# Operands of VectorE moved from SBUF to PSUM in an attention and feed-forward kernel, row additions moved from GpSimd to VectorE, and a second bank for the second products

## The chip, the cores and the metric

One core of one Trainium2 chip. The metric is the device time of one execution in microseconds, the median of three runs. A tile is 128 partitions wide (`P`); PSUM has eight banks of 512 float32 values per partition.

## The reference

Three blocks in a row, float32, batch 2, 768 positions, width 512.

1. Attention with 8 heads of 64. Query and key rows get a bucket from the signs of six projections; only pairs in the same bucket count; then softmax and the product with the values.
2. `u = x + real(fft2(x))` over positions and width; a norm of each row of `u`; `relu(un @ w_ch1) @ w_ch2` with 2048 hidden columns; the result is added to `u`.
3. A gated block: `gelu(x @ w_in)` in two halves, a norm of the second, a product over positions with `w_sg`, a bias, the gate, `w_out`, and the residual.

```python
    X = np.fft.fft(np.fft.fft(x, axis=1), axis=2)
    u = x + np.real(X)
    un = (u - mean(u)) / np.sqrt(var(u) + 1e-06)
    ch = np.maximum(un @ w_ch1, 0.0) @ w_ch2
    return u + ch
```

The weights of blocks 2 and 3 come as 64-bit floats.

## The kernel before, in words

**Precision.** Products of blocks 2 and 3 use pairs of float16, a high and a low part; three products stand for one. Hence the many pairs of a ScalarE copy (`AF.Copy`, high part) and a VectorE subtraction (low part).

**Weights** (`weight`, lines 197 to 239). A load brings 64-bit words into the tile `wide`. Three VectorE instructions make one 32-bit float of the two halves of a word: line 219 shifts and masks the high half, line 220 adds the sign bit, line 221 adds bits of the low half. `w1` is merged in pieces of 1024 columns, `w2` in 16 pieces of 512, `w_in` and `w_out` in pieces of 256. Before the change `t`, the partly merged word, lies in its final place in SBUF. Then ScalarE squares and sums (line 223), and lines 232 and 234 make the high and low parts.

**Attention** (`attention`, lines 360 to 491) goes through 96 items (batch, head, 128 query rows). For each: scores on TensorE (line 387), maximum on VectorE (line 397), exponential on ScalarE (line 399), the float16 pair (lines 244 or 246, and 251 on GpSimd), a transposing DMA (line 438), and the products with the values (lines 455 to 457) into the bank `pav`.

**Transform** (`fft`, lines 494 to 605), per batch. `XU[b]` holds the 768 rows as six tiles; tile `t` and tile `HT + t` belong together. The fold makes their sum `e` and difference `o` and folds the columns (lines 520 to 533). Step 1 (lines 536 to 560) and step 2 (lines 562 to 574) are products with tables. Step 2 gives `p` and `q` in PSUM; ScalarE scales `q` to `qs`; lines 586 and 587 make `d = p - q` and `u = p + q`. They are added to the rows: lines 590 and 591 to tile `A` on VectorE, 595 and 596 to tile `Bt` on GpSimd. Then statistics (lines 599 and 600).

**Norm** (`norm`, lines 607 to 636): a reciprocal root by three Newton steps (`rsqrt`, lines 108 to 118) on one value per row, 6 columns at once for batch 0 and 2 at a time for batch 1. The rows are centred and scaled by a power of two (line 631), split, and transposed by DMA. The block 3 norm calls the same `rsqrt` with one column.

**Feed-forward** (`ch`, lines 639 to 697): chunks of 256 rows. First products (line 657) go into banks of `self.pp`, then lines 663 and 664 make the hidden pair. Second products (line 674) add up 48 matmuls in one bank with the tag `c2`, and line 678 adds the result to `XU`. A chunk has two such groups, one for each 128 rows.

**Order.** `build` merges generators by weights: batch 0's attention with `w1`; then a stream with the rest of the attention and batch 1's transform, a stream with batch 0's transform and feed-forward, and one with `w2`; then batch 1's feed-forward with the block 3 weights; then block 3. `TileContext(nc, schedule_with_timeline_sim=True)` then orders the instructions of each engine by its own model of their times.

**PSUM banks.** While the middle streams run with attention, `self.pp` alternates between two banks; `pa` (tag `pav`) and `pc` (tag `c2`) have one each, and four hold scores. When attention ends, the four go to `pp3`, and `self.pp` rotates over six; `pa` stays allocated with no further use.

Of the kernel before, what the change touches and what calls it, by code (L numbers as in the profile page):

```python
# [9 lines left out]
F32 = mybir.dt.float32  # L10
FR = mybir.dt.float32r
F16 = mybir.dt.float16
I32 = mybir.dt.int32
AF = mybir.ActivationFunctionType
ALU = mybir.AluOpType
# [4 lines left out]
DM, DF, DG = 512, 2048, 1024  # L20
P = 128
# [7 lines left out]
NL = DM // 2 + 1  # L29
# [17 lines left out]
LN1 = (True, False)  # L47
# [54 lines left out]
class Kern:  # L102
    def __init__(self, tc, I, out):
        self.tc, self.nc, self.I, self.out = tc, tc.nc, I, out
        self.W = {}


    def rsqrt(self, pool, x, n):
        nc = self.nc
        y = pool.tile([P, n], F32, tag="rs_y", name="rs_y", bufs=2)  # L110
        t = pool.tile([P, n], F32, tag="rs_t", name="rs_t", bufs=2)
        nc.vector.tensor_scalar(out=y.bitcast(I32), in0=x.bitcast(I32), scalar1=1, scalar2=None, op0=ALU.logical_shift_right)
        nc.vector.tensor_scalar(out=y.bitcast(I32), in0=y.bitcast(I32), scalar1=-1.0, scalar2=float(0x5F3759DF), op0=ALU.mult, op1=ALU.add)
        for _ in range(3):
            nc.vector.tensor_tensor(out=t, in0=y, in1=y, op=ALU.mult)
            nc.vector.scalar_tensor_tensor(out=t, in0=t, scalar=-0.5, in1=x, op0=ALU.mult, op1=ALU.mult)
            nc.vector.scalar_tensor_tensor(out=y, in0=t, scalar=1.5, in1=y, op0=ALU.add, op1=ALU.mult)
        return y

# [77 lines left out]
    def weight(self, pool, nm, src, regions, spare, c, q):  # L197

        nc = self.nc
        wide = src.dtype == mybir.dt.int64  # L200
        src = src.bitcast(I32) if wide else src
        sub = WSUB.get(nm, 4)
        m = c // sub
        n = len(regions)
        s, i = self.sc[nm]
        acc = pool.tile([P, 8], F32, tag="wacc", name="wacc", bufs=1)
        tot = pool.tile([P, 1], F32, tag="wm", name="wm", bufs=1)
        for j in range(n):
            if not wide:
                q.dma_start(out=regions[j], in_=src[:, j * c:(j + 1) * c])  # L210
                yield 0.3
            for hf in range(sub if wide else 0):
                o = j * c + hf * m
                x = self.stp.tile([P, 2 * m], I32, tag="wide", name="wide", bufs=self.wb)
                q.dma_start(out=x, in_=src[:, 2 * o:2 * (o + m)])
                xv = x.rearrange("p (n w) -> p n w", w=2)
                lo, hi = xv[:, :, 0], xv[:, :, 1]
                t = regions[j][:, hf * m:(hf + 1) * m].bitcast(I32)
                nc.vector.tensor_scalar(out=t, in0=hi, scalar1=3, scalar2=0x3FFFFFFF, op0=ALU.logical_shift_left, op1=ALU.bitwise_and)
                nc.vector.scalar_tensor_tensor(out=t, in0=hi, scalar=-0x40000000, in1=t, op0=ALU.bitwise_and, op1=ALU.bitwise_or)  # L220
                nc.vector.scalar_tensor_tensor(out=t, in0=lo, scalar=29, in1=t, op0=ALU.logical_shift_right, op1=ALU.bitwise_or)  # L221
                yield 0.0029 * m
            nc.scalar.activation(spare[:, 0:c], regions[j], AF.Square, accum_out=acc[:, j:j + 1])
            yield 0.0005 * c
        nc.vector.tensor_reduce(tot, acc[:, 0:n], axis=AX.X, op=ALU.add)
        self.norm_pow2(tot, 2.0 ** 54, s, i, self.pc if nm == "w2" else None)
        yield 1.0
        views = []
        dst = spare
        for j in range(n):  # L230
            d = dst[:, 0:c].bitcast(F16).rearrange("p (t c) -> p t c", t=2)
            nc.scalar.activation(d[:, 0, :], regions[j], AF.Copy, scale=i)
            yield 0.0005 * c
            nc.vector.scalar_tensor_tensor(out=d[:, 1, :], in0=regions[j], scalar=i, in1=d[:, 0, :], op0=ALU.mult, op1=ALU.subtract)
            views.append(d)
            dst = regions[j]
            yield 0.0005 * c
        self.W[nm] = views
        self.spare = dst
# [254 lines left out]
    def fft(self, fp, b, unT, up=None):  # L494

        nc, I = self.nc, self.I
# [14 lines left out]
        s, i = self.sx[b]  # L511
        h = DM // 2
# [2 lines left out]
        oe = fp.tile([1, NL], F32, tag="row", name="oe")  # L515
        for t in range(HT):
            A, Bt = XU[:, t], XU[:, HT + t]
            e = fp.tile([P, DM], F32, tag="k2", name="fe", bufs=4)
            o = fp.tile([P, DM], F32, tag="k2", name="fo", bufs=4)
            nc.vector.tensor_tensor(out=e, in0=A, in1=Bt, op=ALU.add)  # L520
            nc.gpsimd.tensor_tensor(out=o, in0=A, in1=Bt, op=ALU.subtract)
            nc.vector.tensor_tensor(out=e[:, 1:h], in0=e[:, 1:h], in1=e[:, DM - 1:h:-1], op=ALU.add)
            nc.scalar.activation(ee[:, t, 0], e[:, 0:NL], AF.Copy, scale=i)
            nc.vector.scalar_tensor_tensor(out=ee[:, t, 1], in0=e[:, 0:NL], scalar=i, in1=ee[:, t, 0], op0=ALU.mult, op1=ALU.subtract)
            if t == 0:
                nc.vector.tensor_tensor(out=oe[:, 1:h], in0=o[0:1, 1:h], in1=o[0:1, DM - 1:h:-1], op=ALU.add)
                nc.vector.tensor_copy(oe[:, 0:1], o[0:1, 0:1])
                nc.vector.tensor_copy(oe[:, h:h + 1], o[0:1, h:h + 1])
                nc.scalar.activation(oeh[0:1, 0], oe, AF.Copy, scale=i[0:1])
                nc.vector.scalar_tensor_tensor(out=oeh[0:1, 1], in0=oe, scalar=i[0:1], in1=oeh[0:1, 0], op0=ALU.mult, op1=ALU.subtract)  # L530
            nc.gpsimd.tensor_tensor(out=o[:, 1:h], in0=o[:, 1:h], in1=o[:, DM - 1:h:-1], op=ALU.subtract)
            nc.scalar.activation(oo[:, t, 0], o[:, 0:h], AF.Copy, scale=i)
            nc.vector.scalar_tensor_tensor(out=oo[:, t, 1], in0=o[:, 0:h], scalar=i, in1=oo[:, t, 0], op0=ALU.mult, op1=ALU.subtract)
            yield 2.0
# [45 lines left out]
        for t in range(HT):  # L580
            p = step2(t * P, P, yc, cl, True)
            q = step2(t * P, P, ys, sl, False)
            qdu = fp.tile([P, 3, NL], F32, tag="k3", name="qdu", bufs=2)
            qs, d, u = (qdu[:, j] for j in range(3))
            nc.scalar.activation(qs, q[:, 0:NL], AF.Copy, scale=s)
            nc.vector.scalar_tensor_tensor(out=d, in0=p[:, 0:NL], scalar=s, in1=qs, op0=ALU.mult, op1=ALU.subtract)
            nc.vector.scalar_tensor_tensor(out=u, in0=p[:, 0:NL], scalar=s, in1=qs, op0=ALU.mult, op1=ALU.add)
            yield 1.6
            A, Bt = XU[:, t], XU[:, HT + t]
            nc.vector.tensor_tensor(out=A[:, 0:NL], in0=A[:, 0:NL], in1=d, op=ALU.add)  # L590
            nc.vector.tensor_tensor(out=A[:, NL:DM], in0=A[:, NL:DM], in1=u[:, h - 1:0:-1], op=ALU.add)
            if t == 0:
                nc.scalar.activation(d[0:1], d3, AF.Copy)
                nc.scalar.activation(u[0:1], d3, AF.Copy)
            nc.gpsimd.tensor_tensor(out=Bt[:, 0:NL], in0=Bt[:, 0:NL], in1=u, op=ALU.add)
            nc.gpsimd.tensor_tensor(out=Bt[:, NL:DM], in0=Bt[:, NL:DM], in1=d[:, h - 1:0:-1], op=ALU.add)
            for n, X in enumerate((A, Bt)):
                st = fp.tile([P, 6], F32, tag="bst", name="bst", bufs=2)
                nc.vector.bn_stats(st, X)
                nc.vector.bn_aggr(mv[:, t, n], st)  # L600
            yield 2.0
            if not LN1[b]:
                yield from self.norm(fp, up, b, unT, mv, (t,))
# [3 lines left out]
    def norm(self, fp, up, b, unT, mv, ts):  # L607
        nc, XU = self.nc, self.XU[b]
        t0, w = ts[0], 2 * len(ts)
        x, e, i, s = (fp.tile([P, w], F32, tag=f"ln{j}", name=f"ln{j}", bufs=1 if LN1[b] else 2) for j in range(4))  # L610
        nc.vector.tensor_scalar(out=x.rearrange("p (a c) -> p a c", c=2), in0=mv[:, t0:ts[-1] + 1, :, 1], scalar1=EPS, scalar2=None, op0=ALU.add)
        nc.vector.tensor_scalar(
            out=e.bitcast(I32), in0=x.bitcast(I32), scalar1=24, scalar2=23, op0=ALU.logical_shift_right, op1=ALU.logical_shift_left
# [1 line left out]
        nc.vector.tensor_scalar(  # L615
            out=i.bitcast(I32), in0=e.bitcast(I32), scalar1=-1.0, scalar2=float(190 << 23), op0=ALU.mult, op1=ALU.add
        )
        rs = self.rsqrt(fp, x, w)
        nc.vector.reciprocal(s, i)
        nc.vector.tensor_tensor(out=self.tok[b][:, 2 * t0:2 * t0 + w], in0=rs, in1=s, op=ALU.mult)  # L620
        yield 0.9
        for t in ts:
            A, Bt = XU[:, t], XU[:, HT + t]
# [15 lines left out]
    def ch(self, hp, b, unT, step, tags=None):  # L639
        nc = self.nc  # L640
# [26 lines left out]
        def c2(n, j, f):  # L667
            w2 = self.W["w2"]
            if f == 0:
                self.c2t = self.pc.tile([P, 512], F32, tag="c2", name="c2")  # L670
            ps = self.c2t
            wv = w2[f // 2].rearrange("p t (k c) -> p t k c", k=2)[:, :, f % 2, :]
            for m, (a, w) in enumerate(HH):
# [141 lines left out]
    def build(self):  # L815
# [3 lines left out]
        with ExitStack() as ctx:  # L819
# [47 lines left out]

            def second():
                yield from att
                c_att.close()  # L870
                c_s2.close()
                pp3 = c_ps.enter_context(tc.tile_pool(name="pp3", bufs=4, space=PSUM))
# [113 lines left out]
```

## Time and profile before

| | |
|---|---|
| median of 3 runs | 722.25 us (721.98 to 722.77) |
| the profiled execution | 724.48 us, span 722.7 us |
| TensorE busy | 645.0 us (89%), 4828 matmuls |
| VectorE busy | 503.9 us (70%), 1095 instructions |
| ScalarE busy | 329.8 us (46%), 517 instructions |
| GpSimd busy | 273.7 us (38%), 232 instructions |
| mean granted TensorE clock | 0.943 |

Busy time is the sum of the spans of an engine's instructions. PE is TensorE, DVE VectorE, ACT ScalarE, POOL GpSimd. A busy engine that waits inside an instruction counts as busy. The granted clock is the share of TensorE's full speed.

### The profile page before, as it was taken

The numbers are of one execution on the slowest core, as the hardware profiler recorded it, in microseconds if no ns is written. First come the engines' busy times: TensorE is split into PE (matmuls) and PEld (weight loads), VectorE is DVE, ScalarE is ACT, GpSimd is POOL, SyncE is SP. The second block draws the span as 40 slices with busy tenths as digits, with TensorE's granted clock in tenths as the row PEclk, the third lists the DMA queues.
The fourth block names the chain that finished last, engine by engine and source line by source line (L and its number), as shares of the span: only waits on it lengthen the run. The fifth ranks groups of instructions, "written<-read, shape, count | busy, mean of one in ns | idle before, by whom it ended". The sixth has DMA issues, their size and how long they took to land.

```text
span 722.7 us, 12521 instructions
## 1 busy us (share of the span) xinstructions
PE 645.0 (89%) x4828; PEld 421.8 (58%) x4828; DVE 503.9 (70%) x1095; ACT 329.8 (46%) x517; POOL 273.7 (38%) x232
## 2 busy tenths in 40 slices
PE   3788987976876578999999999979999999999997
PEld 0666677764563357658865766736668444444443
DVE  6999598658999997745435694867562266777663
ACT  5766687764664556745632421423642044222110
POOL 2568588879486465536455041000000012111000
PEclk8899999996886879999999999989999999999999
DMA  8969787999798989737563036552000012011334
GB/s 310 312 182 213 140 175 143 204 202 259 158 235 169 212 193 211 140 67 152 101 128 108 2 60 221 125 148 91 1 1 1 1 35 53 15 29 18 86 88 117
DMA packets 182428, 92.24 MB, mean 128 GB/s; under 512 B 166240, under 2 KB 167008, under 8 KB 181344
## 3 DMA queue, kind: packets, MB, share of 16 engines
q1 hardware_dynamic: 181792, 91.30, 55.0%
q8 instruction: 38, 0.62, 0.4%
q10 hardware_dynamic: 576, 0.14, 0.1%
q14 instruction: 22, 0.18, 0.1%
HBM read 39.50 MB, written 3.15 MB: 59 GB/s over the span
## 4 chain that ended last, share of the span: by engine, by line
PE 56%; DVE 21%; DMA 12%; POOL 4%; issue 3%; ACT 2%; SPq 0%; DVEq 0%; POOLq 0%; ACTq 0%
PE c L674 13%; PE c L657 12%; PE gi L739 9%; PE sg L762 6%; PE s L387 4%; PE go L779 4%; DMA wide<-w_in 3%; DMA et<-eh 3%; DMA wide<-w 3%; DVE nm L397 2%; DVE w L221 2%; DVE w L220 2%; POOL eh L251 2%; DVE k L258 1%; PE y L542 1%
## 5 line engine op out<-in xcount | busy, mean ns | idle before, releaser
L251 POOL TENSOR_TENSOR eh<-e,eh 128x768 f16<-128x768 f32 x80 | 143.4, 1796 | 53.7 <-ACT eh L244 51.0
L657 PE MATMUL c<-unT,w 128*128 128x256 f16 x1152 | 136.8, 277 | 4.2 <-DVE h L664 4.2
L674 PE MATMUL c<-w,h 128*128 128x512 f16 x576 | 131.8, 384 | 5.3 <-DVE xu L678 5.3
L657 PEld LDWEIGHTS <-w 128*128 128x128 f16 x1152 | 113.0, 99 | 22.6 <-issue 5.3
L387 PE MATMUL s<-k,q 128*128 128x384 f32 x384 | 108.1, 413 | 17.8 <-ACT k L282 7.4
L399 ACT ACTIVATE e<-s,nm 128x768 f32<-128x768 f32 x96 | 85.3, 896 | 55.3 <-DVE nm L397 44.7
L397 DVE TENSOR_REDUCE nm<-s 128x1 f32<-128x768 f32 x96 | 90.3, 948 | 22.6 <-PE s L387 21.5
L674 PEld LDWEIGHTS <-h 128*128 128x128 f16 x576 | 56.2, 99 | 69.6 <-issue 9.2
L755 POOL TENSOR_TENSOR vh<-gv,vh 128x512 f16<-128x512 f32 x12 | 13.9, 1156 | 214.0 <-ACT vh L754 214.0
L387 PEld LDWEIGHTS s<-k,q 128*128 128x128 f32 x384 | 72.0, 211 | 30.1 <-ACT k L282 8.3
L455 PE MATMUL pav<-V,et 128*128 128x65 f16 x480 | 56.4, 199 | 19.2 <-DMA et<-eh 13.8
L664 DVE SCALAR_TENSOR_TENSOR h<-c,h 128x256 f16<-128x256 f32 x96 | 39.8, 419 | 36.3 <-ACT h L663 35.8
L246 POOL TENSOR_SCALAR eh<-e 128x768 f16<-128x768 f32 x48 | 47.9, 999 | 36.8 <-ACT e L399 30.7
L455 PEld LDWEIGHTS <-et 128*128 128x128 f16 x480 | 46.0, 102 | 26.1 <-DMA et<-eh 17.7
L456 PE MATMUL pav<-V,et 128*128 128x64 f16 x480 | 56.2, 197 | 0.0
L457 PE MATMUL pav<-V,et 128*128 128x65 f16 x480 | 56.2, 199 | 0.0
L456 PEld LDWEIGHTS <-et 128*128 128x128 f16 x480 | 46.5, 101 | 7.7 <-issue 6.9
L739 PE MATMUL gi<-in,xT 128*128 128x512 f16 x216 | 50.5, 379 | 0.0
L663 ACT ACTIVATE h<-c 128x256 f16<-128x256 f32 x96 | 34.6, 377 | 34.6 <-PE c L657 34.2
L739 PEld LDWEIGHTS <-xT 128*128 128x128 f16 x288 | 28.2, 98 | 35.0 <-issue 1.1
L457 PEld LDWEIGHTS <-et 128*128 128x128 f16 x480 | 46.5, 101 | 1.5 <-issue 0.8
L762 PE MATMUL sg<-vh,sg 128*128 128x512 f16 x180 | 40.8, 379 | 0.0
(198 smaller groups left out, 1009.9 us busy)
## 6 DMA issues: line engine op xcount, KB each, us to landing
wide<-w SPq DMA_DIRECT2D x8, 1024.0 KB, 8.9
wide<-w SPq DMA_DIRECT2D x16, 512.0 KB, 4.3
x<-qk SPq DMA_DIRECT2D x16, 384.0 KB, 4.5
k<-q SPq DMA_DIRECT2D x26, 192.0 KB, 4.1
wide<-w_in SPq DMA_DIRECT2D x16, 256.0 KB, 3.5
vst<-v SPq DMA_DIRECT2D x8, 396.0 KB, 5.3
y<-ot SPq DMA_DIRECT2D x12, 256.0 KB, 2.3
q<-q SPq DMA_DIRECT2D x13, 192.0 KB, 3.9
```

Source lines behind the costliest of these rows:

```text
L246: self.nc.gpsimd.tensor_scalar(out=out, in0=src, scalar1=scale, scalar2=1.0, op0=ALU.mult, op1=ALU.mult)
L251: (self.nc.vector if eng == "D" else self.nc.gpsimd).tensor_tensor(out=out, in0=a, in1=b, op=ALU.subtract)
L387: nc.tensor.matmul(s[:, hf, 0:HS], q[:, qs], k[:, hf * HS:(hf + 1) * HS], start=n == 0, stop=n == len(pairs) - 1)
L397: nc.vector.tensor_reduce(nm, x["s"], axis=AX.XY, op=ALU.max, negate=True)
L399: nc.scalar.activation(e.rearrange("p (a c) -> p a c", a=2), x["s"], AF.Exp, bias=nm)
L455: nc.tensor.matmul(pv[:, qt, 0:65], et[:, kb, :], V[:, hl, kb, 64:129], start=kb == 0, stop=False)
L456: nc.tensor.matmul(pv[:, qt, 0:64], et[:, kb, :], V[:, hl, kb, 0:64], start=False, stop=False)
L457: nc.tensor.matmul(pv[:, qt, 0:65], et[:, NT + kb, :], V[:, hl, kb, 64:129], start=False, stop=kb == NT - 1)
L657: nc.tensor.matmul(ps[:, 0:step], w[:, a, fo], uT[:, 4 * u + kc, o * P:o * P + step], start=m == 0, stop=m == 11)
L674: nc.tensor.matmul(ps, hs[n, f][:, a, j * P:(j + 1) * P], wv[:, w, :], start=f + m == 0, stop=f == NF - 1 and m == 2)
L739: nc.tensor.matmul(ps, xT[:, 4 * a + kc, :], w_in[kc][:, w, half * DM:(half + 1) * DM], start=n == 0, stop=n == 11)
L762: nc.tensor.matmul(ps, w_sg[kt][:, w, t * P:(t + 1) * P], vh[b][:, kt, a, :], start=n == 0, stop=n == 17)
```

## The change

Six edits.

- `weight`: for `w2` alone the partly merged word lies in a tile of 512 columns with the tag `c2` in PSUM; the third instruction writes the final place in SBUF.
- `rsqrt`: the temporary `t` may be handed in, and the factors are taken in another order (`x*y` times `y` for `y*y` times `x`). `norm` hands in PSUM: `x` and `t` lie in one bank of `self.pp`.
- Fold: `e` lies in a bank of `self.pp` with 257 columns, the other 255 go into `er` in SBUF, by an addition of their own.
- Step 2: `d` and `u` are written over `q` and `p` in their banks.
- The additions to `Bt` go to VectorE.
- `ch`: once the attention is over, every other second product takes the bank of `pa`.

```diff
-    def rsqrt(self, pool, x, n):
+    def rsqrt(self, pool, x, n, t=None):
...
-        t = pool.tile([P, n], F32, tag="rs_t", name="rs_t", bufs=2)
+        t = pool.tile([P, n], F32, tag="rs_t", name="rs_t", bufs=2) if t is None else t
...
-            nc.vector.tensor_tensor(out=t, in0=y, in1=y, op=ALU.mult)
-            nc.vector.scalar_tensor_tensor(out=t, in0=t, scalar=-0.5, in1=x, op0=ALU.mult, op1=ALU.mult)
+            nc.vector.tensor_tensor(out=t, in0=x, in1=y, op=ALU.mult)
+            nc.vector.scalar_tensor_tensor(out=t, in0=t, scalar=-0.5, in1=y, op0=ALU.mult, op1=ALU.mult)
...
-                t = regions[j][:, hf * m:(hf + 1) * m].bitcast(I32)
+                to = regions[j][:, hf * m:(hf + 1) * m].bitcast(I32)
+                t = self.pc.tile([P, 512], F32, tag="c2", name="wt")[:, 0:m].bitcast(I32) if nm == "w2" else to
...
-                nc.vector.scalar_tensor_tensor(out=t, in0=lo, scalar=29, in1=t, op0=ALU.logical_shift_right, op1=ALU.bitwise_or)
+                nc.vector.scalar_tensor_tensor(out=to, in0=lo, scalar=29, in1=t, op0=ALU.logical_shift_right, op1=ALU.bitwise_or)
...
-            e = fp.tile([P, DM], F32, tag="k2", name="fe", bufs=4)
+            e = self.pp.tile([P, 512], F32, tag="p", name="fe")[:, 0:NL]
+            er = fp.tile([P, h - 1], F32, tag="k2", name="fer", bufs=4)
...
-            nc.vector.tensor_tensor(out=e, in0=A, in1=Bt, op=ALU.add)
+            nc.vector.tensor_tensor(out=e, in0=A[:, 0:NL], in1=Bt[:, 0:NL], op=ALU.add)
+            nc.vector.tensor_tensor(out=er, in0=A[:, NL:DM], in1=Bt[:, NL:DM], op=ALU.add)
...
-            nc.vector.tensor_tensor(out=e[:, 1:h], in0=e[:, 1:h], in1=e[:, DM - 1:h:-1], op=ALU.add)
+            nc.vector.tensor_tensor(out=e[:, 1:h], in0=e[:, 1:h], in1=er[:, ::-1], op=ALU.add)
...
-            qdu = fp.tile([P, 3, NL], F32, tag="k3", name="qdu", bufs=2)
-            qs, d, u = (qdu[:, j] for j in range(3))
+            qs = fp.tile([P, NL], F32, tag="k3", name="qs", bufs=2)
+            d, u = q[:, 0:NL], p[:, 0:NL]
...
-            nc.gpsimd.tensor_tensor(out=Bt[:, 0:NL], in0=Bt[:, 0:NL], in1=u, op=ALU.add)
-            nc.gpsimd.tensor_tensor(out=Bt[:, NL:DM], in0=Bt[:, NL:DM], in1=d[:, h - 1:0:-1], op=ALU.add)
+            nc.vector.tensor_tensor(out=Bt[:, 0:NL], in0=Bt[:, 0:NL], in1=u, op=ALU.add)
+            nc.vector.tensor_tensor(out=Bt[:, NL:DM], in0=Bt[:, NL:DM], in1=d[:, h - 1:0:-1], op=ALU.add)
...
-        x, e, i, s = (fp.tile([P, w], F32, tag=f"ln{j}", name=f"ln{j}", bufs=1 if LN1[b] else 2) for j in range(4))
+        e, i, s = (fp.tile([P, w], F32, tag=f"ln{j}", name=f"ln{j}", bufs=1 if LN1[b] else 2) for j in range(3))
+        ps = self.pp.tile([P, 512], F32, tag="p", name="lnp")
+        x, r = (ps[:, 8 * j:8 * j + w] for j in range(2))
...
-        rs = self.rsqrt(fp, x, w)
+        rs = self.rsqrt(fp, x, w, r)
...
-                self.c2t = self.pc.tile([P, 512], F32, tag="c2", name="c2")
+                self.c2n += 1
+                other = self.att_over and self.c2n % 2
+                self.c2t = (self.pa if other else self.pc).tile([P, 512], F32, tag="pav" if other else "c2", name="c2")
...
                 yield from att
+                self.att_over = True
```

## Rows read from the trace of the kernel before

**Rows 1.** Busy time by stage: stretch, its length, engines, granted clock, DMA share, GB/s.

```profile
164.00:290.00 126.00, 92.37 (x828) 64.89 (x827) 116.32 (x186) 70.32 (x109) 81.43 (x63) 0.81 0.92 207
290.00:440.00 150.00, 150.00 (x1313) 104.90 (x1314) 87.13 (x198) 65.16 (x109) 65.57 (x52) 1.00 0.46 94
440.00:579.00 139.00, 132.88 (x879) 86.52 (x878) 78.26 (x227) 44.80 (x92) 0.00 (x0) 0.98 0.25 73
579.00:723.00 144.00, 139.86 (x648) 63.18 (x646) 94.04 (x313) 35.28 (x53) 13.87 (x12) 1.00 0.22 55
```

**Rows 2.** Groups of VectorE, 164 to 290 us: busy us, mean ns, idle before.

```profile
L221 DVE SCALAR_TENSOR_TENSOR w<-wide,w 128x512 int32<-128x512 int32 x16 | 17.7, 1104 | 0.1
L220 DVE SCALAR_TENSOR_TENSOR w<-wide,w 128x512 int32<-128x512 int32 x16 | 16.8, 1051 | 0.1
L219 DVE TENSOR_SCALAR w<-wide 128x512 int32<-128x512 int32 x16 | 9.0, 560 | 2.7 <-DMA wide<-w 2.7
...
L524 DVE SCALAR_TENSOR_TENSOR ee<-fe,ix,ee 128x257 f16<-128x257 f32 x3 | 4.1, 1370 | 0.0
...
L520 DVE TENSOR_TENSOR fe<-xu 128x512 f32<-128x512 f32 x3 | 4.0, 1342 | 0.0
L591 DVE TENSOR_TENSOR xu<-xu,qdu 128x255 f32<-128x255 f32 x3 | 3.7, 1233 | 0.0
...
L590 DVE TENSOR_TENSOR xu<-xu,qdu 128x257 f32<-128x257 f32 x3 | 3.0, 994 | 0.0
L116 DVE SCALAR_TENSOR_TENSOR rs_t<-rs_t,ln 128x6 f32<-128x6 f32 x3 | 2.9, 954 | 0.0
...
L522 DVE TENSOR_TENSOR fe<-fe 128x255 f32<-128x255 f32 x3 | 1.9, 655 | 0.0
...
L117 DVE SCALAR_TENSOR_TENSOR rs_y<-rs_t,rs_y 128x6 f32<-128x6 f32 x3 | 1.4, 480 | 0.0
...
L586 DVE SCALAR_TENSOR_TENSOR qdu<-p,sx,qdu 128x257 f32<-128x257 f32 x3 | 1.4, 468 | 0.0
```

**Rows 3.** Timeline, 184 to 189 us: start us, length us, engine, instruction.

```profile
184.28 0.68 DVE L220 SCALAR_TENSOR_TENSOR w<-wide,w 128x512 int32<-128x512 int32 x1
...
186.54 1.63 POOL L251 TENSOR_TENSOR eh<-e,eh 128x768 f16<-128x768 f32 x1
186.59 2.13 DVE L221 SCALAR_TENSOR_TENSOR w<-wide,w 128x512 int32<-128x512 int32 x1
```

**Rows 4.** TensorE's waits, 440 to 585 us: total us, times, longest.

```profile
PE c L674 <- DVE xu L678: 5.3, 2, 4.4
PE gi L739 <- DVE xu L678: 0.8, 1, 0.8
```

**Rows 5.** Timeline of VectorE ahead of TensorE's longer wait.

```profile
481.94 0.29 DVE L219 TENSOR_SCALAR in<-wide 128x256 int32<-128x256 int32 x1 [0.70 <-DMA wide<-w_in]
...
482.61 0.75 DVE L678 SCALAR_TENSOR_TENSOR xu<-c,tok,xu 128x512 f32<-128x512 f32 x1
```

**Rows 6.** Groups of VectorE over the whole span, for prices.

```profile
L766 DVE SCALAR_TENSOR_TENSOR t<-t,bB,gu 128x512 f32<-128x512 f32 x12 | 9.0, 752 | 0.4
...
L678 DVE SCALAR_TENSOR_TENSOR xu<-c,tok,xu 128x512 f32<-128x512 f32 x12 | 9.0, 746 | 23.7 <-PE c L674 23.7
...
L765 DVE TENSOR_TENSOR t<-sg,gB 128x512 f32<-128x512 f32 x12 | 8.3, 692 | 15.3 <-PE sg L762 15.3
...
L116 DVE SCALAR_TENSOR_TENSOR rs_t<-rs_t,ve 128x1 f32<-128x1 f32 x36 | 5.7, 159 | 1.2
```

**Rows 7.** Group of GpSimd, 164 to 290 us.

```profile
L596 POOL TENSOR_TENSOR xu<-xu,qdu 128x255 f32<-128x255 f32 x3 | 2.5, 821 | 1.4 <-DVE qdu L586 1.4
```

**Rows 8.** Timeline of VectorE, batch 0's step 2 and root.

```profile
202.65 0.47 DVE L587 SCALAR_TENSOR_TENSOR qdu<-p,sx,qdu 128x257 f32<-128x257 f32 x1
...
205.48 0.99 DVE L591 TENSOR_TENSOR xu<-xu,qdu 128x255 f32<-128x255 f32 x1
...
235.28 0.14 DVE L611 TENSOR_SCALAR ln<-mv 128x6 f32<-128x6 f32 x1
...
255.77 0.17 DVE L117 SCALAR_TENSOR_TENSOR rs_y<-rs_t,rs_y 128x6 f32<-128x6 f32 x1
```

More of the change, by code (lines that the diff above doesn't have):

```diff
@@ L105, in __init__ @@
         self.W = {}
-    def rsqrt(self, pool, x, n):
+        self.c2n, self.att_over = 0, False
+    def rsqrt(self, pool, x, n, t=None):
         nc = self.nc
         y = pool.tile([P, n], F32, tag="rs_y", name="rs_y", bufs=2)
-        t = pool.tile([P, n], F32, tag="rs_t", name="rs_t", bufs=2)
+        t = pool.tile([P, n], F32, tag="rs_t", name="rs_t", bufs=2) if t is None else t
         nc.vector.tensor_scalar(out=y.bitcast(I32), in0=x.bitcast(I32), scalar1=1, scalar2=None, op0=ALU.logical_shift_right)
```

## The prediction

> **What bounds the kernel now.** I read the busy table by stage first, cut where the TensorE row of the page changes character. Four stages matter [rows 1]. From 290 us on TensorE sets the time: it is busy 150.0 of 150, 132.9 of 139 and 139.9 of 144 us, at a granted clock of 1.00, 0.98 and 1.00. From 164 to 290 us it isn't: it works 92.4 of 126 us, at 0.81. There batch 1's attention, batch 0's transform and the merging of the words of `w2` run together, and VectorE is busy 116.3 of 126 us. The DMA share is 0.92 too, which makes some 116 us of transfers. Before 164 us nothing is changed: `w1` still merges in SBUF. So the reader should look for two things: what VectorE does between 164 and 290, and where TensorE still waits after 440.
>
> The groups of VectorE in that stretch answer the first [rows 2]. Instructions with two SBUF tensors take far more than their size asks: 1.05 and 1.10 us for 512 elements, 0.99 and 1.23 us for 257 and 255, 0.95 us for six elements (line 116). In the same stretch line 586, one PSUM and one SBUF tensor of 257, takes 0.468. The timeline shows why [rows 3]: the same merge step takes 0.68 us alone, and 2.13 us where it starts 0.05 us behind a GpSimd add that itself lasts 1.63. VectorE stands until GpSimd lets go. [...]
>
> The second: after 440 us TensorE's waits for VectorE come to 5.3 us at line 674, in two pieces, the longer 4.4, and 0.8 at line 739 [rows 4]. Line 674 wants the only `c2` bank, which line 678 must empty. Line 678 stands in VectorE's queue among the merges of `w_in`, and those wait for their loads [rows 5].
>
> **The change part by part**, in the stretch from 164 to 290, in VectorE time. Prices for one PSUM and one SBUF tensor: 0.692 us for 512 elements without a scalar pointer, 0.746 with one, so the pointer costs 0.054 [rows 6]; 0.468 for 257 with a pointer, so 0.41 without.
>
> Words of `w2`, 16 halves: lines 220 and 221 now cost 16.8 + 17.7 = 34.5 us; 32 times 0.692 is 22.1, so -12.4. Line 219 (0.560) has no row with a PSUM output. Its ends are no change and the full 0.692; I take the latter, as nearest in size: +2.1. Together -10.3. All 16 share the one `c2` bank, so the steps of two halves can't overlap any more; VectorE runs them in turn anyway, and nothing else wants that bank until `w2` is ready.
>
> Fold, three tiles: line 520 (1.342) becomes two adds, both still with two SBUF inputs. Between 0.41 alone and the 0.99 of line 590 I take 0.99, since GpSimd works beside them: 6 x 0.99 - 4.0 = +1.9. Line 522 falls from 0.655 to 0.41 (-0.7 in three), line 524 from 1.370 to 0.468 (-2.7). Together -1.5.
>
> Row additions: lines 590 and 591 fall from 0.994 and 1.233 to 0.41 each (-1.8 and -2.5). Six additions come from GpSimd, 6 x 0.41 = +2.5. Together -1.8. GpSimd loses them, three of 0.82 us [rows 7] and three of about that width, some 5 us, which shortens its hold on the others. VectorE's queue gets them ahead of the statistics, which had waited for GpSimd.
>
> Root: each of its three-input steps then has one SBUF tensor. Lines 116 and 117 (0.954 and 0.480) fall to the 0.159 of the same step where nothing disturbs it [rows 6]: -2.4 - 1.0 = -3.4. The other order of factors changes no count.
>
> Sum: -10.3 - 1.5 - 1.8 - 3.4 = -17.0 us of VectorE. What a VectorE write to PSUM costs isn't in the trace. At best it is nothing. At worst the steps that write PSUM (lines 220, 522 and 116) stay at what they take now; they are 5.7 + 0.7 + 2.4 = 8.8 us of the sum, so the relief is 8.2 to 17.0. I take 17.0: a read from PSUM shows no surcharge, 0.746 (line 678) against 0.752 for the like with two SBUF tensors (line 766) [rows 6].
>
> How much of it shortens the stage? VectorE idles 9.7 us of 126, so it alone would let all 17 through. The transfers don't shrink: 0.92 of 126 us is 116, so about 10 us is what there is before they bind. Attention's transposes could slide into the next stage, where the share is 0.46 [rows 1]. I take -10, with -3 and -17 as ends. From 290 on TensorE is full, so its work simply starts earlier and the gain stays.
>
> Two banks for second products: `att_over` is set before batch 1's part, so the 5.3 us of line 674 go; the other bank has been empty for a whole group of 48 matmuls. The loads of `w_in` then are late for nobody on TensorE until the last stage. The 0.8 us at line 739 I leave. -5.3, with -3 and -6.1 as ends.
>
> After 384 us, batch 1's transform runs beside a full TensorE. Its VectorE savings are worth nothing there, and its longer held banks may cost: six banks rotate, so I put +1 for all of them (0 to +4).
>
> Total -10 - 5.3 + 1 = -14.3. The profiled execution took 724.48 us (span 722.7), 2.2 over the median of 722.25. It should come to 710.2, and the median to 708.0.
>
> **The rivals.**
>
> Transfers hold the stage (0.17). If the 0.92 is already what the transfers can do with their waits, VectorE's relief turns into waiting for loads, and only the banks remain: 722.25 - 5.3 + 1 = 718. For it speaks the share; against it that after 290 us, with the same transposes, it is 0.46, and that VectorE is just as full.
>
> PSUM writes are dear (0.08): a relief of 8.2 instead of 17.0, and the same 10/17 of it gained, is 4.8; with the banks -9.1, or 713. [...]
>
> Banks held too long (0.10), the one that ends slower. In the stage at issue two banks serve the fold, both steps of the transform, the root and attention's norm. The pair `p`, `q` was free when line 587 ended, at 203.1; now it is held past line 591, which ended at 206.5, and two more additions of 0.41: 4.2 us longer [rows 8], three times 12.6. The root holds a bank from 235.3 to 255.9 [rows 8], when first products want both: up to 4. The fold's first sum may wait for one tile's chain, 1.34 + 0.66 + 1.37 = 3.4. TensorE takes its instructions in order, so attention waits behind. That is 20 us, against 15.3 saved: about 727 if none hides. It decides once more than 15.3 of the 20 are exposed. Against it: TensorE is idle 33.6 us of this stage already, and such waits fall into that.
>
> It doesn't do what it says (0.05): the stretching stays, and only the additions count, 2.1 + 1.9 + 2.5 = +6.5, against -5.3: some 722 to 724.
>
> **How the numbers follow.** The forecast has 0.60. About 0.2% is what a measurement of this kernel can tell from no change. Faster takes the forecast, the dear writes and most of the first rival, 0.83; the same, the unchanged case and the bad end of the first, 0.07; slower, the held banks, 0.10. The range: below, the whole 17 and 6.1, 722.25 - 23.1 = 699; above, the first rival at 718 with a little more of the bank waits, 719. Outside lie the held banks, the unchanged case and a sliver below.
>
> **What would show it.** Right: `w2`'s line 220 and 221 steps near 0.69 us with hardly any above 0.8; lines 522, 524, 590, 591 at 0.41 to 0.47; root steps near 0.16; six more additions on VectorE and none of these on GpSimd; the first second product some 10 us earlier than 289; no wait for line 678 at line 674. Wrong: these fall but the stage stays 126 us long and `w2`'s first step waits for its load (transfers); the steps that write PSUM stay near 1 us (dear writes); TensorE waits in the transform for lines 590 to 596 of the new kernel (banks). The order of instructions on each queue is drawn up anew for the changed kernel, which can shift a few us either way.

## The result, and the profile after

The changed kernel takes 713.93 us (median of 4 runs, 712.84 to 714.82) against 722.12 for the kernel before beside it (719.14 to 722.77). The ratio is 0.9861, with an interval of 0.9823 to 0.9899: faster by 1.4%, which is 10 us by the ratio and 8 between the medians. The forecast was 708.0 with a range of 699 to 719. The profiled execution took 714.82 us, its span is 713.0.

Busy time by stage, the kernel after, in the cuts of [rows 1]:

```profile
164.00:290.00 126.00, 95.75 (x915) 69.11 (x914) 111.17 (x201) 78.84 (x118) 81.24 (x65) 0.86 1.10 226
290.00:440.00 150.00, 148.51 (x1245) 101.98 (x1244) 83.51 (x210) 56.26 (x98) 47.19 (x37) 1.00 0.42 86
440.00:579.00 139.00, 133.69 (x882) 86.85 (x880) 79.43 (x239) 48.22 (x96) 0.00 (x0) 0.99 0.22 60
579.00:713.00 134.00, 130.20 (x604) 58.82 (x601) 88.65 (x291) 30.91 (x48) 13.87 (x12) 0.99 0.24 58
```

From 290 us on TensorE sets the time as it did. In the first stretch it works 95.75 us at a granted clock of 0.86, before 92.37 at 0.81 (means of two levels: in cuts of 0.5 us the clock is 0.50 or 1.00 in 239 of 252 before and in 242 of 252 after). Busy time times clock estimates its work at full speed (the clock is a mean over the whole stretch, idle time included): 82.3 us against 74.8. So some 7.5 us more of it is done by the same moment, and is spared later, where the clock is 0.99 to 1.00. The busy time is only 3.4 us longer; the rest is the higher clock. It isn't that this execution was ahead already: cut 3 us earlier, from 161 to 287 us, the kernel after has the same 95.75 us at 0.86.

Groups of VectorE in the stretch from 164 to 290 us of the kernel after (against [rows 2]):

```profile
L221 DVE TENSOR_SCALAR wt<-wide 128x512 int32<-128x512 int32 x16 | 11.0, 686 | 1.5 <-DMA wide<-w 1.4
L222 DVE SCALAR_TENSOR_TENSOR wt<-wide,wt 128x512 int32<-128x512 int32 x16 | 10.9, 683 | 0.1
L223 DVE SCALAR_TENSOR_TENSOR w<-wide,wt 128x512 int32<-128x512 int32 x16 | 10.8, 672 | 0.1
L637 DVE TENSOR_SCALAR un<-xu,mv,ln 128x512 f32<-128x512 f32 x6 | 10.2, 1704 | 0.0
...
L524 DVE TENSOR_TENSOR fer<-xu 128x255 f32<-128x255 f32 x2 | 2.5, 1262 | 0.0
...
L523 DVE TENSOR_TENSOR fe<-xu 128x257 f32<-128x257 f32 x2 | 1.6, 824 | 0.0
...
L528 DVE SCALAR_TENSOR_TENSOR ee<-fe,ix,ee 128x257 f16<-128x257 f32 x3 | 1.4, 466 | 0.0
...
L526 DVE TENSOR_TENSOR fe<-fe,fer 128x255 f32<-128x255 f32 x3 | 1.3, 420 | 0.0
L599 DVE TENSOR_TENSOR xu<-xu,p 128x257 f32<-128x257 f32 x3 | 1.2, 415 | 1.8 <-ACT p L598 1.8
...
L595 DVE TENSOR_TENSOR xu<-xu,p 128x255 f32<-128x255 f32 x3 | 1.2, 405 | 0.0
...
L117 DVE SCALAR_TENSOR_TENSOR lnp<-lnp,rs_y 128x6 f32<-128x6 f32 x3 | 0.5, 163 | 0.0
...
L118 DVE SCALAR_TENSOR_TENSOR rs_y<-lnp,rs_y 128x6 f32<-128x6 f32 x3 | 0.5, 153 | 0.0
```

The three word steps (now lines 221 to 223) take 32.7 us against 43.5: the two with two inputs 21.7 for 34.5, the one with one input 11.0 for 9.0. Lines 526, 528, the additions (594, 595, 599, 600) and the root are at the prices of the sum. The two adds of the fold's first sum, both with two SBUF tensors, stay at 0.82 and 1.26 us. The row that speaks against the change is line 637, the centring: 10.2 us in six, against 5.8 in the kernel before. Its longest one in the timeline, VectorE first, then GpSimd:

```profile
246.84 4.64 DVE L637 TENSOR_SCALAR un<-xu,mv,ln 128x512 f32<-128x512 f32 x1
```

```profile
246.84 1.15 POOL L639 TENSOR_TENSOR hl<-un,hl 128x512 f16<-128x512 f32 x1
247.95 3.25 POOL L253 TENSOR_TENSOR eh<-e,eh 128x768 f16<-128x768 f32 x2
```

It starts with a GpSimd step and ends 0.3 us after the third of them in a row.

TensorE's waits from 440 to 585 us, the kernel after (against [rows 4]):

```profile
PE c L663 <- DVE h L670: 2.5, 2, 2.0
PE pb L137 <- issue: 2.0, 1, 2.0
PE gi L747 <- DVE xu L686: 0.8, 1, 0.8
```

The wait of second products (now line 682) for line 686 is gone. In its place first products (line 663) wait for `h`, and the small product of a weight's norm (`pb`, line 137) for something that this view doesn't name ("issue"; the second bank's experiment below shows what): 4.5 us against 5.3.

### The profile page after: what moved, and what is told of

Same layout as the page of the kernel before. It is cut to its first block, busy times and chain, and to the rows that moved or that the text cites. A ratio compares the mean times of both kernels' runs of the same rounds, so it can differ in the third digit from the quotient of the medians.

```text
span 713.0 us, 12541 instructions
## 1 busy us (share of the span) xinstructions
PE 636.5 (89%) x4828; PEld 418.1 (59%) x4828; DVE 495.8 (70%) x1113; ACT 330.9 (46%) x517; POOL 258.6 (36%) x220
## 4 chain that ended last, share of the span: by engine, by line
PE 57%; DVE 20%; DMA 14%; POOL 3%; issue 3%; ACT 1%; SPq 1%; DVEq 0%; POOLq 0%; ACTq 0%
PE c L663 13%; PE c L682 12%; PE gi L747 9%; PE sg L770 7%; DMA et<-eh 5%; PE go L787 4%; PE s L389 4%; DVE nm L399 3%; DMA wide<-w_in 3%; DMA wide<-w 3%; PE y L546 2%; DVE k L260 2%; POOL eh L253 2%; DMA wide<-w_out 2%; DMA x<-qk 1%
## 5 line engine op out<-in xcount | busy, mean ns | idle before, releaser
L253 POOL TENSOR_TENSOR eh<-e,eh 128x768 f16<-128x768 f32 x80 | 137.7, 1725 | 50.2 <-ACT eh L246 47.4
L682 PE MATMUL c<-w,h 128*128 128x512 f16 x576 | 129.5, 379 | 0.0
L389 PE MATMUL s<-k,q 128*128 128x384 f32 x384 | 104.4, 402 | 14.9 <-ACT k L284 11.6
L248 POOL TENSOR_SCALAR eh<-e 128x768 f16<-128x768 f32 x48 | 51.3, 1070 | 45.0 <-ACT e L401 37.2
```

The lines of the kernel that those rows point to most:

```text
L248: self.nc.gpsimd.tensor_scalar(out=out, in0=src, scalar1=scale, scalar2=1.0, op0=ALU.mult, op1=ALU.mult)
L253: (self.nc.vector if eng == "D" else self.nc.gpsimd).tensor_tensor(out=out, in0=a, in1=b, op=ALU.subtract)
L389: nc.tensor.matmul(s[:, hf, 0:HS], q[:, qs], k[:, hf * HS:(hf + 1) * HS], start=n == 0, stop=n == len(pairs) - 1)
L682: nc.tensor.matmul(ps, hs[n, f][:, a, j * P:(j + 1) * P], wv[:, w, :], start=f + m == 0, stop=f == NF - 1 and m == 2)
```

## The experiments

Every ratio is to the kernel before, timed beside it; the row `after` is the result above. The span of each profile is cut here at two events of the trace: the first fold (`fo` on GpSimd), up to about which the order of every engine is the same before and after, and the first weight load of the last stage's product `gi`, after which it takes 145.1 to 145.3 us in all of them. "Fold to end" is from the first fold to the last attention product, "end to `gi`" the rest.

| kernel | ratio (95%) | fold at | fold to end | end to `gi` | fold to `gi` |
|---|---|---|---|---|---|
| before | 1 | 165.5 | 218.2 | 193.9 | 412.1 |
| banks_alone | 1.0008 (0.9979 to 1.0036) | 166.7 | 217.7 | 195.1 | 412.7 |
| no_words | 0.9962 (0.9932 to 0.9991) | 163.5 | 217.9 | 193.3 | 411.2 |
| words_alone | 0.9849 (0.9807 to 0.9892) | 162.5 | 208.9 | 194.8 | 403.8 |
| no_banks | 0.9903 (0.9867 to 0.9939) | 164.6 | 209.9 | 194.7 | 404.5 |
| words_banks | 0.9887 (0.9866 to 0.9907) | 164.3 | 207.6 | 196.9 | 404.4 |
| words_rootfold | 0.9872 (0.9840 to 0.9905) | 161.2 | 210.7 | 193.8 | 404.5 |
| words_root | 0.9884 (0.9848 to 0.9919) | 165.0 | 210.2 | 195.1 | 405.3 |
| words_du | 0.9951 (0.9932 to 0.9971) | 165.5 | 214.6 | 194.5 | 409.1 |
| words_adds | 0.9951 (0.9921 to 0.9980) | 162.1 | 203.1 | 202.4 | 405.5 |
| after_du_sbuf | 0.9921 (0.9900 to 0.9941) | 165.9 | 211.0 | 196.1 | 407.1 |
| after | 0.9861 (0.9823 to 0.9899) | 162.7 | 212.2 | 193.1 | 405.3 |
| before_halfin | 0.9990 (0.9964 to 1.0016) | 165.8 | 218.1 | 191.0 | 409.1 |
| banks_halfin | 0.9942 (0.9916 to 0.9967) | 164.9 | 217.6 | 188.9 | 406.5 |

The column "fold at" moves by 5.5 us between profiles. Nearly all changed instructions come behind it (ahead of it lie only the first tile's additions of `e`), so 2.9 of the 9.7 us between the two profiled spans count as variation.

**The two large edits, each alone and each taken out.** `words_alone` and `banks_alone` are the kernel before with one edit; `no_words` and `no_banks` are the kernel after without it.

```diff
 words
-                t = regions[j][:, hf * m:(hf + 1) * m].bitcast(I32)
+                to = regions[j][:, hf * m:(hf + 1) * m].bitcast(I32)
+                t = self.pc.tile([P, 512], F32, tag="c2", name="wt")[:, 0:m].bitcast(I32) if nm == "w2" else to
 banks
-                self.c2t = self.pc.tile([P, 512], F32, tag="c2", name="c2")
+                self.c2t = (self.pa if other else self.pc).tile([P, 512], F32, tag="pav" if other else "c2", name="c2")
```

> The kernel before with the partly merged words of w2 in PSUM alone. Steps 220 and 221 at 0.69 us, about 10 us of VectorE less between 164 and 290 us. Theory A (transposing transfers and GpSimd's hold on other instructions take up part of the relief): 3 to 5 us of gain, 717 to 719 us. Rival B (VectorE's relief goes through in full, and something else of the change costs): 9 to 10 us, 712 to 713 us. Rival C (nothing: the stage is held by the transfers alone): 722 us.

> The kernel before with the second bank for second products alone. The 5.3 us of waits at the second products should go in any case. Theory A (the waits are passed on: VectorE's queue still stands behind the loads of the block 3 weights, and first products wait there instead): 1 us or less of gain, about 721.5 us, with new waits of TensorE for line 664's successor of 2 us or more after 440 us. Rival B (the gain is real and is lost elsewhere in the changed kernel): about 717 us.

> The changed kernel with the words of w2 merged in SBUF as before. Theory A: loses 3 to 5 us of the 8, about 717 to 719 us. Rival B: loses 9 to 10, about 723 us. Rival C: no loss, 714 us, so the transform's edits carry the gain.

> The changed kernel without the second bank for second products; everything else of the change stays. Theory A: within 1.5 us of the changed kernel, 713.5 to 715.5 us, with a few us of waits at the second products back and those for the hidden pair gone. Rival B: 5 us slower than the changed kernel, about 719 us.

Measured: 0.9849, 1.0008, 0.9962 and 0.9903. The words carry the gain: 8.3 us from fold to `gi` in the profile, all of it before the end of attention, and as much by the ratio as the whole change. That is rival B of `words_alone`. Taking them out costs some 7 us and taking the banks out some 3 (by the ratios), each between the two theories. The other edits without the words still stand at 0.9962, with an interval clear of 1: a small gain, which doesn't add to that of the words. The stage from 164 to 290 us of `words_alone`:

```profile
164.00:290.00 126.00, 96.75 (x905) 67.86 (x903) 115.04 (x196) 78.07 (x121) 80.64 (x67) 0.88 0.99 220
```

VectorE is as full as before [rows 1]; it does other work in the time that the words leave. The second bank by itself is worth nothing, and the waits after 384 us of `banks_alone` show why:

```profile
PE pb L137 <- issue: 3.6, 1, 3.6
PE c L658 <- DVE h L665: 2.2, 1, 2.2
PE gi L742 <- DVE xu L681: 0.8, 1, 0.8
```

5.8 us stand where 5.3 stood [rows 4]. What was late was VectorE's queue, not the bank. The view names no releaser for `pb`, the larger part. But that product reads `wm`, the sum of a weight's squares, which VectorE makes (line 226) when the merge of `w_in` is through, and it starts 0.10 us after that sum ends (timeline of VectorE and TensorE):

```profile
482.35 0.29 DVE L220 TENSOR_SCALAR in<-wide 128x256 int32<-128x256 int32 x1 [1.47 <-DMA wide<-w_in]
...
486.25 0.29 DVE L220 TENSOR_SCALAR out<-wide 128x256 int32<-128x256 int32 x1 [1.25 <-DMA wide<-w_out]
...
486.92 0.15 DVE L226 TENSOR_REDUCE wm<-wacc 128x1 f32<-128x4 f32 x1
487.17 0.56 PE L137 MATMUL pb<-wm,ones 128*128 128x1 f32 x2 [3.61 <-issue]
```

The same 0.10 us stands in all five kernels that have the second bank and all loads (in the kernel after from 477.16 to 477.26). So TensorE itself comes to a product that needs the merged `w_in`, and the loads make it late. In the kernel after, the `h` for which TensorE waits longest (2.0 us, to 492.05) stands behind work of VectorE's own: of a load only 0.26 us is left there, and the low part of `w_in` (line 236) takes 1.28 (timeline of VectorE):

```profile
488.83 0.30 DVE L221 TENSOR_SCALAR out<-wide 128x256 int32<-128x256 int32 x1 [0.26 <-DMA wide<-w_out]
489.04 0.75 DVE L222 SCALAR_TENSOR_TENSOR out<-wide,out 128x256 int32<-128x256 int32 x2
489.71 0.42 DVE L223 SCALAR_TENSOR_TENSOR out<-wide,out 128x256 int32<-128x256 int32 x1
490.05 1.28 DVE L236 SCALAR_TENSOR_TENSOR in<-in,i_in,in 128x1024 f16<-128x1024 f32 x1
491.24 0.42 DVE L223 SCALAR_TENSOR_TENSOR out<-wide,out 128x256 int32<-128x256 int32 x1
491.58 0.75 DVE L670 SCALAR_TENSOR_TENSOR h<-c,h 128x256 f16<-128x256 f32 x2
```

**Half the loads of the last weights.** Every second piece of `w_in` and `w_out` isn't loaded; its merge uses the piece that is there, so half of these weights are other data. `before_halfin` is the kernel before so cut, `banks_halfin` has the second bank too.

```diff
-                x = self.stp.tile([P, 2 * m], I32, tag="wide", name="wide", bufs=self.wb)
-                q.dma_start(out=x, in_=src[:, 2 * o:2 * (o + m)])
+                if nm not in ("in", "out") or hf % 2 == 0:
+                    x = self.stp.tile([P, 2 * m], I32, tag="wide", name="wide", bufs=self.wb)
+                    q.dma_start(out=x, in_=src[:, 2 * o:2 * (o + m)])
```

> The kernel before with only every other piece of w_in and w_out loaded; the merges of the other pieces use the piece that is there, so half of those weights are other data. If VectorE's merges that stand for their loads are what delays line 678 (5.3 us of TensorE's wait at line 674), the wait falls to 0 to 1 us and the time by some 4 to 5 us, 0.993 to 0.995. If VectorE is late there with its own work, the wait stays at 4 to 6 us and the ratio is 1.00.

> The same cut of the loads of w_in and w_out, with the second bank for second products added. With full loads the second bank gave 1.0008, its wait at the second products replaced by waits of first products for h (2.2 us) and of the weights' norm product (3.6 us). If loads that hold up VectorE's queue are what passes the wait on, both are gone here (under 1 us in all) and the ratio equals that of the cut without the second bank, within 0.3%. If something else of the second bank costs time, this run is slower than that one by 0.3% or more.

Waits from 384 to 600 us, first of `before_halfin`, then of `banks_halfin`:

```profile
PE c L675 <- DVE xu L679: 2.1, 2, 1.2
PE c L658 <- DVE h L665: 0.9, 1, 0.9
PE gi L740 <- DVE xu L679: 0.8, 1, 0.8
```

```profile
PE c L659 <- DVE h L666: 1.6, 2, 1.0
PE c L659 <- DVE x_s L129: 0.9, 1, 0.9
PE gi L743 <- DVE xu L682: 0.8, 1, 0.8
```

Both expectations missed in part. With fewer loads line 675's wait falls to 2.1 us, not to 1, and the ratio stays at 0.999, though the profile is 3.0 us shorter from fold to `gi`. The cut didn't take the loads out of the way: the longer piece of that wait, 1.2 us at 453.82, comes behind a wait of VectorE for `w_in`:

```profile
450.19 0.49 DVE L220 TENSOR_SCALAR in<-wide 128x256 int32<-128x256 int32 x2 [6.02 <-DMA wide<-w_in]
```

With the second bank the passed-on waits fall from 5.8 to 2.5 us, the `pb` one is gone, and the ratio is 0.9942. So the bank is worth some 0.5% once loads hold VectorE up less (the intervals of the two cut kernels still touch), and nothing that shows while they do. The two had been expected equal. Their waits nearly are, 3.0 and 2.5 us. What differs more between the two profiles is TensorE's granted clock from 440 to 470 us, 0.94 without the second bank and 1.00 with it:

```profile
440.00:470.00 30.00, 27.86 (x204) 20.41 (x202) 23.39 (x82) 10.48 (x24) 0.00 (x0) 0.94 0.49 157
440.00:470.00 30.00, 28.54 (x227) 22.08 (x226) 24.26 (x86) 11.51 (x27) 0.00 (x0) 1.00 0.58 166
```

**The transform's edits on top of the words.** `words_root` hands `rsqrt` its PSUM bank, `words_rootfold` adds the fold, `words_banks` has the words and the second bank.

```diff
 root
+        ps = self.pp.tile([P, 512], F32, tag="p", name="lnp")
+        x, r = (ps[:, 8 * j:8 * j + w] for j in range(2))
 fold
-            e = fp.tile([P, DM], F32, tag="k2", name="fe", bufs=4)
+            e = self.pp.tile([P, 512], F32, tag="p", name="fe")[:, 0:NL]
```

> The words edit and the root in PSUM, nothing else. The sum reckoned 3.4 us of VectorE for the root; if it counts as the words' relief did, the ratio is 0.980 to 0.982 and the transposes start some 3 us earlier after the fold than the 68.6 us of words alone. If the bank held from the root's first step to its last takes it back, the first products or attention's norm wait and the ratio is 0.985 to 0.988. Words with root and fold stood at 0.987, so a 0.982 here would put the loss on the fold.

> The kernel before with the words of w2, the root and the fold in PSUM; d and u in SBUF and the additions to Bt on GpSimd as before. Theory A (the transform's edits hold the two banks too long, above all the pair p and q): near the words alone, ratio 0.982 to 0.988 to the kernel before (710 to 714 us), the three steps of d some 5 to 7 us apart as with the words alone. Rival B (the fold's or the root's bank is what delays): as the whole change or worse, 0.988 to 0.993 (714 to 718 us). Rival C (their 5 us of relief go through in full): 0.978 (707 us).

> The kernel before with the words of w2 in PSUM and the second bank for second products. The words alone still have 4.4 us of waits at the second products. Theory A (passed on to first products, whose emptying stands behind the loads of the block 3 weights): 0.983 to 0.987, within 2 us of the words alone. Rival B (they go): 0.978 to 0.980, 707 to 708 us.

0.9884, 0.9872 and 0.9887: none is better than the words alone, and the three intervals overlap with theirs. Relief that VectorE gets beyond the words isn't turned into time that these runs can tell.

**The row additions.** `words_du` has `d` and `u` in PSUM and all additions on VectorE; `words_adds` the additions alone, with `d` and `u` in SBUF; `after_du_sbuf` is the kernel after with `d` and `u` back in SBUF.

```diff
 du
-            qs, d, u = (qdu[:, j] for j in range(3))
+            d, u = q[:, 0:NL], p[:, 0:NL]
 adds
-            nc.gpsimd.tensor_tensor(out=Bt[:, 0:NL], in0=Bt[:, 0:NL], in1=u, op=ALU.add)
+            nc.vector.tensor_tensor(out=Bt[:, 0:NL], in0=Bt[:, 0:NL], in1=u, op=ALU.add)
```

> The kernel before with the words of w2 in PSUM, d and u over q and p in their banks, and the additions to Bt on VectorE; root and fold as before. Theory A: worse than the words alone by 2 to 5 us, 0.988 to 0.992 (714 to 717 us), with the second step of d 10 us or more behind the first. Rival B: as the words alone or a little better, 0.981 to 0.986 (709 to 713 us).

> The words edit and the additions to Bt on VectorE, with d and u left in SBUF. Measured so far against before: words alone 0.985, words with d and u in PSUM and the additions on VectorE 0.995. If it is the additions in VectorE's queue that take the words' gain back, this run is near 0.995 too and batch 0's transposes start some 78 us or more after the fold (words alone: 68.6). If it is the long hold of the banks p and q, this run stays near 0.985 with the transposes at 69 to 72 us after the fold. Two-SBUF additions on VectorE beside GpSimd cost about 1.0 us each, six more of them.

> The changed kernel with d and u in SBUF as before; the additions to Bt stay on VectorE. Only the time for which p and q hold their banks differs, and the additions have two SBUF inputs again. Theory A (bank hold): 2 to 4 us faster than the changed kernel, ratio to the kernel before 0.981 to 0.984, first transposed rows of batch 0 some 5 us earlier. Rival B (the six additions on VectorE are the cost): no faster than the changed kernel, 0.986 to 0.991. Rival C (the stretched additions cost more than the hold): slower than the changed kernel by 2 us or more.

`words_du` and `words_adds` both stand at 0.9951, 1% above the words alone; either theory of `words_du` had less. So the banks' hold isn't needed for the loss: the additions on VectorE bring it without. Within the whole change it is otherwise: `after_du_sbuf`, at 0.9921, is slower than the kernel after by 0.6% (rival C; the intervals just don't overlap), so there `d` and `u` in PSUM help. Why the kernel after, with the same additions, doesn't lose the 1% stays open. The loss of `words_du` isn't the time of the added steps, though. From batch 0's first `d` to its first centring, `words_alone` takes 29.3 us (196.9 to 226.2) and `words_du` 36.9 (200.3 to 237.2). The groups of VectorE in these two stretches, `words_alone` first:

```profile
L398 DVE TENSOR_REDUCE nm<-s 128x1 f32<-128x768 f32 x7 | 6.6, 942 | 0.0
...
L591 DVE TENSOR_TENSOR xu<-xu,qdu 128x257 f32<-128x257 f32 x3 | 3.6, 1215 | 0.0
```

```profile
L398 DVE TENSOR_REDUCE nm<-s 128x1 f32<-128x768 f32 x11 | 10.5, 951 | 1.8 <-PE s L388 1.7
...
L591 DVE TENSOR_TENSOR xu<-xu,p 128x257 f32<-128x257 f32 x3 | 1.2, 413 | 0.0
```

The twelve additions take 4.9 us, the six of `words_alone` 5.6. What stands between is four more maxima of attention (3.9 us), one more half of a word merge (2.0) and waits. The order of VectorE, drawn anew, lets attention go first. That the later transform is the loss isn't shown: in the kernel after the first transpose of `un` comes 84.0 us after the fold (68.6 in `words_alone`) and fold to `gi` is 405.3 all the same. The profiled execution of `words_adds` (714.47) lies far under its median of 718.72, so its row doesn't show what its median lost; its first transpose comes 73.4 us after the fold, where 78 had been expected.

## Why the prediction was right, and where not

**VectorE's terms held, one by one**, in the stretch from 164 to 290 us. Words: 43.5 to 32.7, -10.8 for -10.3 (in it the step with one input, +2.0 for +2.1). Fold: line 524 of before saves 2.7, line 522 0.7, and the split sum costs 0.82 + 1.26 - 1.34 = 0.74 a tile, together -1.2 for -1.5. Additions: 6.7 us become 12 of 0.41, -1.8 for -1.8. Root: 4.3 to 1.0, -3.3 for -3.4. In all -17.1 for -17.0. For steps with two inputs a write to PSUM shows no surcharge (0.683 us for the one that writes it, 0.672 for the one that writes SBUF), so the second rival falls. A PSUM source shows none either: both steps read one, and the undisturbed step in SBUF took 0.68 too [rows 3]. The word step with one input does pay for its place in PSUM (shortest, median and longest of 16 in ns, before and after):

```profile
L219 DVE TENSOR_SCALAR w<-wide x16: 407/419/1079, 182.6 to 278.5; 128x512 int32<-128x512 int32 x16
L221 DVE TENSOR_SCALAR wt<-wide x16: 676/684/695, 175.3 to 274.1; 128x512 int32<-128x512 int32 x16
```

Its mean of 0.560, from which the sum starts, mixed undisturbed steps of 0.41 with stretched ones of up to 1.08: in SBUF it was faster and could be held up, in PSUM it is neither. The fourth rival falls with the rest, since the stretching went.

**The -10 of 17** came out as a number, not for its reason, and that is luck. The step was that the stage gets shorter, with the first second product some 10 us earlier than 289. It came 2.4 us earlier, and counted from the first fold 0.5 us later (before, then after):

```profile
288.89 0.38 PE L674 MATMUL c<-w,h 128*128 128x512 f16 x1
```

```profile
286.53 0.38 PE L682 MATMUL c<-w,h 128*128 128x512 f16 x1
```

The stage kept its length; TensorE got more done in it, for the larger part by its higher clock, a term that the sum didn't have. The words alone brought 8.3 us of their 10.8 in the profile, about 11 by the ratio, and on top of them the other 6 us brought nothing that these runs can tell. The step gave as the limit a DMA share of 0.92 that transfers could not exceed. It rose to 1.10, with 226 GB/s for 207, and the words' first step waited 1.4 us for its loads, 2.7 before. So 0.92 was no ceiling. Among TensorE's waits, the one that grew most is for attention's transposing DMA (waits from 160 to 290 us; the first line is of the kernel before, the second of the one after):

```profile
PE pav L455 <- DMA et<-eh: 4.0, 4, 2.0
```

```profile
PE pav L457 <- DMA et<-eh: 14.6, 7, 5.4
```

It is 9.8 us in `words_alone` and 12.2 in `words_banks`, but 7.3 in `words_rootfold`, and already 3.7 to 7.1 in the four kernels that are alike in this stretch (`before`, `banks_alone` and the two with halved loads); the kernel before also waits 5.1 us at the same product for line 464, which is gone. So a form of the first rival may set the limit now, through the transposes and not through the loads of `w2`. The size of the wait doesn't follow the measured times, and no run here takes the transposes or those loads away, so this is argued and not shown.

**The banks' -5.3 was the mis-sized term.** It measured +0.6 us alone (-1.5 to +2.6); on top of the other edits the two ratios, 0.9903 and 0.9861, don't separate. The mechanism that failed is "The loads of `w_in` then are late for nobody on TensorE until the last stage": they were late for the product `pb`, which needs the merged `w_in` (3.6 of the 5.8 us in `banks_alone`), and the rest of the wait went to `h` in VectorE's queue. With 0 in its place the sum gives 722.25 - 10 + 1 = 713.25; 713.93 was measured.

**Banks held too long** was there, and small: in `no_words` TensorE waits 2.7 us at step 2 for the last addition to release the bank, and 0.5 at `pb`; the kernel after shows no such wait. 12.6 us had been put on it. That TensorE takes its instructions in order, on which this rival rests, fits a wait of the kernel before: TensorE stood 4.4 us, to 483.41, at a second product, while the first products that it took up at 496.25 had had their rows since 441.0 (the last transpose of `unT` was issued at 437.3 and landed 3.7 us later at most).

The root's, the fold's and the additions' edits could be left out: the words alone measured 0.9849 against 0.9861, a difference that the intervals don't separate.

## What to carry to other kernels

Price an edit by instruction from rows of the same shape, and then ask per edit, not for the sum, who uses the time set free: here the first 10 us of VectorE turned into time, and the next 6 on top of them did not. Before a wait on a buffer is cleared with a second buffer, look at what stands ahead of its releaser in that queue: here it was waits for loads, and the next product that needed the same data (`pb`, 3.6 us in `banks_alone`) and the next consumer in the queue (`h`, 2.2 us) inherited the wait. Where a view gives "issue" as the reason, look up what the waiting instruction reads. Cut spans at events, so that what varies ahead of the change isn't counted as its effect.

## What the runs showed of the hardware

More than half of what TensorE gained in the stage was clock, by the estimate above: 0.81 to 0.86 with 92.4 to 95.8 us of 126 busy. Over the span its busy time fell from 645.0 to 636.5 us while its idle time hardly moved (77.7 to 76.5), so in these profiles nearly the whole gain stands in the time that its instructions take.

VectorE seems to stand behind more than one GpSimd step: one step of line 637 took 4.64 us (the shortest of the six took 0.50), while GpSimd went through three in a row, although it reads one SBUF tensor of full size. The prediction had reckoned with such stretching only for steps with two SBUF tensors. Line 219 reads one too, and its rows agree with line 637: of its 16 steps of 512 columns in the kernel before, the six above 0.5 us (0.58 to 1.08) all began while a GpSimd step ran, of the ten of 0.41 to 0.42 us only one did. What holds a step there, no run shows, and the 4.64 us behind several GpSimd steps are a single case.
